# Three of five token blocks of the second expert turned by the DMA queue instead of the matrix engine

## The chip, the cores and the metric

The kernel runs on one core of one Trainium2 chip. Its time is device microseconds (us) of one execution. Before the change three runs gave 709.59, 711.19 and 712.39 us; the median is 711.19 us. One more execution was profiled, and all durations below are from it.

The engines are named as in the profile: PE is the matrix engine, PEld its weight loads, DVE the vector engine, ACT the scalar engine, POOL GpSimd, SP the engine that issues most DMAs. A `q` behind a name (SPq) is the engine's instruction queue, where DMAs are issued.

## The reference

The first half is attention over 8 batches, 8 heads, 576 positions and 64 values a head: a softmax over positions averaged by four, repeated four times, plus a softmax over the neighbours with |i - j| < 4. The sum, 4608 tokens of 512 values, is `x` of the second half, a mixture of eight experts with room for 576 tokens each:

```python
logits = x @ w_gate
order = np.argsort(-flat)                    # best pair of token and expert first
for idx in order:
    tok, e = (int(idx) // E, int(idx) % E)
    if assigned[tok] >= 0 or counts[e] >= cap:
        continue
    assigned[tok] = e
    counts[e] += 1
for e in range(E):
    mask = assigned == e
    h = np.maximum(x[mask] @ w1[e], 0.0)     # 576 x 512 by 512 x 1024
    out[mask] = h @ w2[e]                    # 576 x 1024 by 1024 x 512
```

## The kernel before

**Stages.** Attention writes `x` to DRAM (`x_dram`) and the logits to SBUF. Then a routing phase finds which expert fills up first and the numbers of its 576 tokens; each later phase finds the next expert and runs beside the previous expert's matmuls. Experts run one after another. "The second expert" below is the one with `i == 1` in the loop of `moe_attention`; its tokens and weights are fetched and prepared while the first expert's last matmuls run.

**One expert.** `weights` loads 4 MB on SP's queue; `split` makes of each piece two fp16 parts, `wh` (ACT, L1200) and the remainder `wl` (DVE, L1202, two instructions of 512 columns a piece). `gather` fetches the tokens' rows in five blocks (four of 128 rows and one of 64) into `xg` by indirect DMA from POOL (L1217). A block must be turned, so that the 512 values lie on the partitions, and split into a high and a remainder part, giving `xt`. There are two ways. `piece` turns a block on PE, four 128x128 fp32 transposes (L1234) into PSUM, and then ACT writes the high part (L1238) and DVE the remainder (L1239). `piece_dma` splits first, ACT (L1245) and DVE (L1246) into `xs`, and then SP issues one DMA that turns both parts (L1248). Experts one and two use `piece`, the others `piece_dma`.

**The two layers.** In `mlp` the first layer goes over eight slices `f` of 128 hidden columns. Each has two sums in PSUM tile `pH`, over tokens 0 to 255 (12 matmuls of 256 columns, L1279) and over tokens 256 to 575 (12 matmuls of 320 columns). The 12 are four slices of the depth by three products: high by high, high weight by remainder of x, remainder of the weight by high x. The list `seq` takes the three products in turn for each slice of depth. The list `late`, used by the first expert for `f < 2`, takes the four high products first, then the four with the weight's remainder, then the four with x's remainder; there the sums over 256 tokens of `f` 0 and 1 come before both sums over 320. The results go to `ht`, high part by ACT (L1303), remainder by DVE (L1306). The second layer goes over the five blocks `c` (L1320) into `pX`, ACT scales into `y` (L1327), for block 4 DVE adds its second half (L1329), POOL scatters the rows (L1330).

**What sets the order.** Each engine takes its instructions in program order, and a scheduler places them by priority and by the hints in the code. `in2` says behind which block of the previous expert's second layer the next expert's blocks are prepared: for the first expert the table `GET0` says blocks 0 and 1 behind block 3, blocks 2 to 4 behind block 4. The routing phase's own matmuls on PE (L871 counts against thresholds `level` or `cmp`, L889 and L917 broadcasts) stand between the layers' matmuls; each L871 waits for a compare on DVE (L822, which makes `cmp`), and the next L889 waits for three `less` and one `flag` on DVE (L881, L884). `val` and `ol` (L905, L1051) close the first count and start the second.

Of the kernel before, what the change touches and what calls it, by code (L numbers as in the profile page):

```python
# [734 lines left out]
W1S, W2S, XM = 64.0, 64.0, 8.0  # L735
# [413 lines left out]
class Experts:  # L1149
# [58 lines left out]
    def gather(self, idx, first, second=False):  # L1208
# [15 lines left out]
        def piece(c):  # L1224
# [12 lines left out]
            with self.tc.high_priority():  # L1237
                nc.scalar.activation(hi, p[:, :, :n], AF.Copy, scale=XM)  # L1238
                self.lows.append(nc.vector.scalar_tensor_tensor(lo, p[:, :, :n], XM, hi, op0=OP.mult, op1=OP.subtract))  # L1239

        def piece_dma(c):
            s0, n = SL[c]
            xs = self.wk.tile([128, 2, HD], F16, name="xs", bufs=XSB)
            with self.tc.high_priority():
                nc.scalar.activation(xs[:n, 0], xgs[c][:n], AF.Copy, scale=XM)  # L1245
            getattr(nc, LOE).scalar_tensor_tensor(xs[:n, 1], xgs[c][:n], XM, xs[:n, 0], op0=OP.mult, op1=OP.subtract)  # L1246
            with self.tc.high_priority():
                self.sent = nc.sync.dma_start_transpose(xt[:, :, :, s0:s0 + n].rearrange("p a d s -> p (a d) s"),  # L1248
                                            xs[:n].rearrange("p a d -> p (a d)"))

        return xt, piece if first or second else piece_dma

# [8 lines left out]

    def mlp(self, w, xt, idx, in1, in2, first=False):
        nc = self.nc
# [12 lines left out]
        def product(f, p, s):  # L1276
            s0, s1 = CUT[s]
            for j, (d, a, b) in enumerate(late if first and f < 2 else seq):
                mm = nc.tensor.matmul(p[:, s, :s1 - s0], w[d][a][:, 128 * f:128 * f + 128], xt[:, b, d, s0:s1],  # L1279
                                      start=j == 0, stop=j == len(seq) - 1)  # L1280
                self.products.append(mm)
                mark(mm, (s1 - s0) / 2400)
            return mm

        ph = {}
        for f in range(8):
            for z in (0, 1) if first and f == 0 else () if first and f == 1 else (f,):
                ph[z] = self.ps.tile([128, 2, 512], F32, name="pH", bufs=2)
# [53 lines left out]
GET = {0: (0, 1), 1: (2, 3), 2: (4,)}  # L1342
GET0 = {3: (0, 1), 4: (2, 3, 4)}
BEHIND = ((1, 6), (2, 2))
# [10 lines left out]
def moe_attention(tc, q, k, v, wg, w1, w2, cst, out):  # L1355
    nc = tc.nc
    with ExitStack() as top:
# [13 lines left out]
        with ExitStack() as ctx:  # L1371
# [21 lines left out]
            for i in range(E):  # L1393
# [29 lines left out]

                ex.mlp(w, xt, idx, in1, in2, i == 0)
                if i == 0:
# [66 lines left out]
```

## Time and profile before

| | us |
|---|---|
| median of three runs | 711.19 |
| the profiled execution | 709.79 |
| its span, first to last instruction | 708.1 |
| PE busy in the span | 649.8 (92%) |
| DVE busy | 533.6 (75%) |
| ACT busy | 337.7 (48%) |

The profiled execution took 1.69 us more than its span and lies 1.40 us under the median. By stage, PE is busy 222.42 of the first 250 us (attention), 14.13 of the next 30 (first routing phase, clock granted 0.61 of full speed on average), 65.47 of 280 to 347 (first expert), 55.68 of 347 to 405 (second expert) and 292.12 of 405 to 698 (the other six). Busy means that at least one instruction of the engine is under way; matmuls overlap, so the distance between two starts tells more than a duration. In the rows below the number in brackets is the idle time of the engine before an instruction, and what released it. A granted clock of 1.00 is 2.4 GHz, 0.50 is 1.2 GHz.

### The profile page before, as it was taken

Reading aid. Unit: us, or ns where it says so; the run is one execution under the profiler, and the core shown is the slowest. Engines: PE = TensorE matmul, PEld = TensorE weight load, DVE = VectorE, ACT = ScalarE, POOL = GpSimd, SP = SyncE. Lnnn points to the kernel's source line nnn. Section 1 sums busy time; section 2 is a strip of 40 time slices with the busy share of each in tenths; the row PEclk is TensorE's granted clock in tenths of the full one; section 3 lists DMA queues with packets and bytes.
Section 4 is the critical chain, followed back from the end, with each engine's and each line's share of the span. In section 5 each row is a group of like instructions: output and inputs, shape, how many; then the busy total and the mean of one; then the engine's idle time right before and its main releaser. Section 6 shows DMA issues by size and latency. Waiting matters only on the chain.

```text
span 708.1 us, 21934 instructions
## 1 busy us (share of the span) xinstructions
PE 649.8 (92%) x8938; PEld 451.0 (64%) x8938; DVE 533.6 (75%) x1562; ACT 337.7 (48%) x650; POOL 232.7 (33%) x303
## 2 busy tenths in 40 slices
PE   6888999889999845999999999999999999999994
PEld 4667878778787733774574575575674674755741
DVE  5798889987989977887889697797797876634500
ACT  4567778787785521532532443443444424424410
POOL 4865374644737420402402303204104106202011
PEclk9899999999999975999999999999999999999997
DMA  9967859777785632605507617638348269814001
GB/s 263 245 157 218 227 159 245 205 205 202 197 238 160 192 117 89 218 1 181 192 1 283 157 43 269 129 116 229 95 183 204 55 233 198 313 35 100 1 31 38
DMA packets 132157, 113.73 MB, mean 161 GB/s; under 512 B 81240, under 2 KB 109912, under 8 KB 132056
## 3 DMA queue, kind: packets, MB, share of 16 engines
q1 hardware_dynamic: 124760, 90.76, 45.0%
q0 software_dynamic: 6432, 20.98, 9.5%
q8 instruction: 71, 1.16, 0.7%
q10 hardware_dynamic: 864, 0.58, 0.3%
q14 instruction: 30, 0.25, 0.1%
HBM read 85.74 MB, written 19.46 MB: 149 GB/s over the span
## 4 chain that ended last, share of the span: by engine, by line
PE 45%; DVE 22%; issue 17%; ACT 5%; DMA 5%; POOL 4%; SPq 1%; ACTq 0%; POOLq 0%; DVEq 0%
PE pH L1279 13%; PE pX L1320 11%; PE g L574 3%; PE pR L871 2%; DVE wl L1202 2%; PE g L327 2%; POOL out_dram L1330 2%; DVE x L453 2%; PE g L552 2%; PE g L592 2%; PE s L532 1%; DVE qt L311 1%; POOL xg L1217 1%; PE g L407 1%; PE pH L1186 1%
## 5 line engine op out<-in xcount | busy, mean ns | idle before, releaser
L1279 PE MATMUL pH<-xt,wh 128*128 128x256 f16 (+1 forms) x1024 | 191.3, 286 | 1.2 <-ACT xt L1238 0.5
L1320 PE MATMUL pX<-wh,ht 128*128 128x512 f16 (+1 forms) x640 | 178.0, 379 | 0.0
L1279 PE MATMUL pH<-xt,wl 128*128 128x320 f16 (+1 forms) x512 | 144.6, 286 | 0.0
L1320 PEld LDWEIGHTS <-ht 128*128 128x128 f16 (+1 forms) x960 | 82.6, 100 | 93.9 <-issue 3.8
L1320 PE MATMUL pX<-wl,ht 128*128 128x512 f16 (+1 forms) x320 | 117.6, 379 | 0.0
L1279 PEld LDWEIGHTS <-wh 128*128 128x128 f16 x1024 | 97.5, 98 | 30.2 <-issue 5.7
L1330 POOL DMA_INDIRECT out_dram<-y,idx x40 | 43.0, 1074 | 177.8 <-ACT y L1327 153.5
L1303 ACT ACTIVATE ht<-pH 128x512 f16<-128x512 f32 (+1 forms) x128 | 45.5, 407 | 112.5 <-PE pH L1279 112.5
L1202 DVE SCALAR_TENSOR_TENSOR wl<-nat,wh 128x512 f16<-128x512 f32 x128 | 83.5, 687 | 14.9 <-ACT wh L1200 8.3
L1327 ACT ACTIVATE y<-pX 128x512 f32<-128x512 f32 (+1 forms) x40 | 23.8, 594 | 103.4 <-PE pX L1320 54.3
L1306 DVE SCALAR_TENSOR_TENSOR ht<-pH,ht 128x512 f16<-128x512 f32 (+1 forms) x128 | 52.3, 450 | 24.4 <-ACT ht L1303 23.9
L1200 ACT ACTIVATE wh<-nat 128x1024 f16<-128x1024 f32 x64 | 67.3, 1053 | 4.1 <-DMA nat<-in_moe_w_dram 4.1
L1217 POOL DMA_INDIRECT xg<-x_dram,idx x40 | 42.5, 1062 | 61.9 <-DVE used L1100 33.4
L1279 PEld LDWEIGHTS <-wl 128*128 128x128 f16 x512 | 49.9, 98 | 12.7 <-issue 0.8
L563 ACT COPY pt<-g 64x512 f32<-64x512 f32 x72 | 41.8, 581 | 28.8 <-PE g L552 27.8
L574 PE MATMUL g<-vw,pt 128*64 128x65 f32 x1152 | 45.5, 229 | 5.6 <-issue 2.7
L574 PEld LDWEIGHTS g<-vw,pt 128*64 128x64 f32 x1152 | 39.6, 142 | 12.7 <-issue 6.6
L327 PE MATMUL g<-ident,nat 128*128 128x128 f32 x256 | 40.4, 283 | 3.9 <-DMA nat<-in_q_dram 3.3
L313 ACT COPY kt<-g 64x512 f32<-64x512 f32 (+1 forms) x60 | 38.3, 639 | 6.2 <-PE g L327 5.2
L1246 DVE SCALAR_TENSOR_TENSOR xs<-xg,xs 128x512 f16<-128x512 f32 (+1 forms) x30 | 20.3, 688 | 26.8 <-ACT xs L1245 15.7
L1019 POOL MEMSET f<- 128x1 bf16 x8 | 0.8, 106 | 116.3 <-DVE sumf L925 44.2
L300 POOL TENSOR_TENSOR gtmp<-kt 128x576 f32<-128x576 f32 x14 | 16.1, 1147 | 61.4 <-ACT kt L313 43.6
(221 smaller groups left out, 1153.0 us busy)
## 6 DMA issues: line engine op xcount, KB each, us to landing
nat<-in_moe_w_dram SPq DMA_DIRECT2D x28, 1024.0 KB
vw<-in_v_dram SPq DMA_DIRECT2D x136, 78.0 KB
x_dram<-x SPq DMA_DIRECT2D x36, 256.0 KB
nat<-in_q_dram SPq DMA_DIRECT2D x32, 256.0 KB
nat<-in_k_dram SPq DMA_DIRECT2D x32, 256.0 KB
nat<-in_v_dram SPq DMA_DIRECT2D x28, 256.0 KB
up<-up_dram SPq DMA_DIRECT2D x9, 256.0 KB
nat<-in_moe_w_dram SPq DMA_DIRECT2D x4, 512.0 KB
```

The costliest lines, as they stand in the source:

```text
L313: self.nc.scalar.copy(out, in_)
L327: nc.tensor.transpose(p[:, a, :, fp], src[:, 4 * hh + 2 * a + s, 2 * fp:2 * fp + 2].rearrange("p f d -> p (f d)"), self.ident)
L563: self.nc.scalar.copy(out, in_)
L574: nc.tensor.matmul(o[64 * i:64 * i + 64, 65 * h:65 * h + 65], pt[:, 2 * (h % 2) + i, 2 * g + h // 2].rearrange("p b q -> p (b q)"), self.v ...
L1200: nc.scalar.activation(hi, r, AF.Copy, scale=sc)
L1202: nc.vector.scalar_tensor_tensor(lo[:, a:a + LOP], r[:, a:a + LOP], sc, hi[:, a:a + LOP], op0=OP.mult, op1=OP.subtract)
L1217: self.fetched = nc.gpsimd.indirect_dma_start(out=xg[:n], out_offset=None, in_=self.x, in_offset=bass.IndirectOffsetOnAxis(ap=idx[:n, c:c ...
L1279: mm = nc.tensor.matmul(p[:, s, :s1 - s0], w[d][a][:, 128 * f:128 * f + 128], xt[:, b, d, s0:s1], start=j == 0, stop=j == len(seq) - 1)
L1303: last = nc.scalar.activation(hi, q, AF.Relu)
L1306: low = nc.vector.scalar_tensor_tensor(lo, q, 0.0, hi, op0=OP.max, op1=OP.subtract)
L1320: mm = nc.tensor.matmul(p[o:o + m], ht[:, f, h0:h0 + m], w[4 + f // 2][b][:, 512 * (f % 2):512 * (f % 2) + 512], start=j < parts, stop=j > ...
L1330: i = nc.gpsimd.indirect_dma_start(out=self.out, in_=y[:n], in_offset=None, out_offset=bass.IndirectOffsetOnAxis(ap=idx[:n, c:c + 1], axis=0))
```

## The change

Blocks 2, 3 and 4 of the second expert are prepared by `piece_dma`; blocks 0 and 1 stay with `piece`. All five are now asked for behind block 3 of the first expert's second layer (`GET0`). A hint keeps ACT's part of `piece_dma` behind the high part of block 1. And the second expert too uses the order `late` for `f < 2`, with both sums over 256 tokens ahead of both sums over 320. Behind the edits every line number of the changed kernel is larger: L1279 is L1284 there, L1246 is L1249, L1248 is L1251, L1306 is L1311, L1329 is L1334.

```diff
-                nc.scalar.activation(hi, p[:, :, :n], AF.Copy, scale=XM)
+                self.high = nc.scalar.activation(hi, p[:, :, :n], AF.Copy, scale=XM)
...
         def piece_dma(c):
...
-                nc.scalar.activation(xs[:n, 0], xgs[c][:n], AF.Copy, scale=XM)
+                half = nc.scalar.activation(xs[:n, 0], xgs[c][:n], AF.Copy, scale=XM)
+            if second:
+                self.tc.add_manual_dep(half.ins, self.high.ins.name, mybir.DependencyInfo(
+                    mybir.DependencyClass.NoSync, mybir.DependencyReason.DATA), reason="behind")
...
-        return xt, piece if first or second else piece_dma
+        if first:
+            return xt, piece
+        return xt, (lambda c: (piece_dma if c in SENT2 else piece)(c)) if second else piece_dma
...
-    def mlp(self, w, xt, idx, in1, in2, first=False):
+    def mlp(self, w, xt, idx, in1, in2, first=False, two=False):
...
-            for j, (d, a, b) in enumerate(late if first and f < 2 else seq):
+            for j, (d, a, b) in enumerate(late if two and f < 2 else seq):
...
-            for z in (0, 1) if first and f == 0 else () if first and f == 1 else (f,):
+            for z in (0, 1) if two and f == 0 else () if two and f == 1 else (f,):
...
-GET0 = {3: (0, 1), 4: (2, 3, 4)}
+GET0 = {3: (0, 1, 2, 3, 4)}
+SENT2 = (2, 3, 4)
...
-                ex.mlp(w, xt, idx, in1, in2, i == 0)
+                ex.mlp(w, xt, idx, in1, in2, i == 0, i < 2)
```

On PE, where the second expert's first layer begins, the kernel before has this; `wh_6902` to `wh_7014` are the four depth slices of its weights, `level_82` the thresholds of the routing phase that runs beside it.

```order
L1234 MATMUL pH<-ident,xg 128x128 x4
L1234 MATMUL pX<-ident,xg 128x64 x4
L871 LDWEIGHTS level_82
...
L1279 MATMUL pH<-xt,wl_6969 128x256
L1234 MATMUL pH<-ident,xg 128x128 x4
L1279 LDWEIGHTS wh_7014
...
L889 MATMUL pR<-flag_5872,one 128x8
...
L1279 MATMUL pH<-xt,wl_7015 128x256
L1279 LDWEIGHTS wh_6902
L1279 MATMUL pH<-xt,wh_6902 128x320
```

Blocks 2 and 4 are turned ahead of the first layer, block 3 inside the first sum, and the sum over 320 tokens follows after 12 matmuls of 256 columns. In the changed kernel the same engine has, from the end of the first layer's 24th matmul of 256 columns:

```order
L1284 MATMUL pH<-xt,wh_7026 128x256
L871 LDWEIGHTS cmp_7116
L871 MATMUL pR<-oh,cmp_7116 128x32
...
L889 LDWEIGHTS one
L889 MATMUL pR<-flag_5874,one 128x8
L1284 LDWEIGHTS wh_6902
L1284 MATMUL pH<-xt,wh_6902 128x320
```

The three turns are gone, the 18 matmuls on `level_82` have moved up behind the turn of block 1, and nine L871 and one L889 of the next routing step stand together between the last 256-column and the first 320-column matmul. Before, these nine stood behind 12 matmuls of 256 columns and 7 of 320, and the L889 another 3 and 5 later. From the nine L871 on `cmp_7217` on (the second compare after `ol`) the routing's matmuls stand behind the same numbers of layer matmuls in both kernels.

On DVE the stretch from the remainder of block 1 on is, as a difference:

```order
 L1239 SCALAR_TENSOR_TENSOR xt<-pH,xt 128x4x128
-L1329 SCALAR_TENSOR_TENSOR y<-pX,y 64x512
...
 L881 TENSOR_TENSOR less<-cap,pR 64x8
+L1249 SCALAR_TENSOR_TENSOR xs<-xg,xs 128x512
 L884 TENSOR_TENSOR flag_5872<-pR,less 64x8
...
+L1249 SCALAR_TENSOR_TENSOR xs<-xg,xs 128x512
+L1334 SCALAR_TENSOR_TENSOR y<-pX,y 64x512
 L894 TENSOR_REDUCE nj<-pR 128x1
...
+L1249 SCALAR_TENSOR_TENSOR xs<-xg,xs 64x512
```

The remainders of blocks 2, 3 and 4 now stand among the routing step's small operations, the 64-row block behind the addition for `y`, and all of them ahead of the threshold and the compare that make `cmp_7116`. On SP the three turning DMAs stand behind the second expert's four weight loads and ahead of the third expert's.

## Rows read from the trace of the kernel before

**Rows 1.** Timeline of PE: start, us, engine, line, operation, [idle before <-releaser].
```profile
343.44 0.66 PE L1234 MATMUL pH<-ident,xg 128*128 128x128 f32 x4
...
345.66 0.66 PE L1234 MATMUL pH<-ident,xg 128*128 128x128 f32 x4
...
346.63 0.62 PE L871 MATMUL pR<-oh,level 128*128 128x16 bf16 x18
347.10 0.38 PE L1279 MATMUL pH<-xt,wh 128*128 128x256 f16 x2
...
348.08 0.60 PE L1234 MATMUL pH<-ident,xg 128*128 128x128 f32 x4
...
349.36 0.30 PE L1279 MATMUL pH<-xt,wh 128*128 128x320 f16 x1 [0.33 <-ACT xt L1238]
350.09 0.30 PE L1279 MATMUL pH<-xt,wh 128*128 128x320 f16 x1 [0.43 <-DVE xt L1239]
...
350.90 0.38 PE L871 MATMUL pR<-oh,cmp 128*128 128x32 bf16 x9
...
352.13 0.17 PE L889 MATMUL pR<-flag,one 128*128 128x8 bf16 x1
...
359.29 0.60 PE L871 MATMUL pR<-ol,level 128*128 128x16 bf16 x18 [0.19 <-DVE ol L1051]
```

**Rows 2.** Timeline of DVE, same stretch.
```profile
344.85 0.68 DVE L1239 SCALAR_TENSOR_TENSOR xt<-pH,xt 128x512 f16<-128x512 f32 x1
...
350.05 0.75 DVE L822 TENSOR_TENSOR cmp<-xh,thr 128x1152 bf16<-128x1152 int16 x1
351.32 0.16 DVE L881 TENSOR_TENSOR less<-cap,pR 32x8 f32<-32x8 f32 x1 [0.51 <-PE pR L871]
...
351.90 0.15 DVE L884 TENSOR_TENSOR flag<-pR,less 32x8 bf16<-32x8 f32 x1
...
358.94 0.30 DVE L1051 TENSOR_TENSOR ol<-oh,e 128x288 bf16<-128x288 bf16 x1
```

**Rows 3.** Timeline of ACT, same stretch.
```profile
345.81 0.59 ACT L1327 ACTIVATE y<-pX 64x512 f32<-64x512 f32 x1 [1.08 <-PE pX L1320]
...
352.01 0.71 ACT L1303 ACTIVATE ht<-pH 128x512 f16<-128x512 f32 x2 [2.69 <-PE pH L1279]
```

**Rows 4.** Instructions that write tiles xs and xt by the DMA way: ns min/median/max.
```profile
L1245 ACT ACTIVATE xs<-xg x30: 612/629/631, 388.1 to 643.2; 128x512 f16<-128x512 f32 x24, 64x512 f16<-64x512 f32 x6
L1246 DVE SCALAR_TENSOR_TENSOR xs<-xg,xs x30: 683/688/693, 388.7 to 643.8; 128x512 f16<-128x512 f32 x24, 64x512 f16<-64x512 f32 x6
L1248 SPq DMA_TRANSPOSE xt<-xs x30: 1222/1293/2304, 389.5 to 644.6; - x30
```

**Rows 5.** Timeline of SP: the last 64-row turn, issued alone.
```profile
644.56 1.22 SPq L1248 DMA_TRANSPOSE xt<-xs  x1
```

**Rows 6.** Last busy quarter microsecond of its transfer: busy by engine, clock, DMA share, GB/s.
```profile
646.50:646.75 0.25, 0.25 (x3) 0.10 (x1) 0.00 (x0) 0.00 (x0) 0.00 (x0) 1.00 0.64 93
```

**Rows 7.** Half microseconds at a gather's end, same columns.
```profile
387.50:388.00 0.50, 0.50 (x4) 0.22 (x3) 0.41 (x4) 0.00 (x0) 0.33 (x1) 1.00 0.03 8
```

**Rows 8.** Timeline of ACT: waits for a gather and for a turning DMA.
```profile
388.06 0.63 ACT L1245 ACTIVATE xs<-xg 128x512 f16<-128x512 f32 x1 [4.97 <-DMA xg<-x_dram,idx]
...
446.10 0.63 ACT L1245 ACTIVATE xs<-xg 64x512 f16<-64x512 f32 x1 [0.80 <-DMA xt<-xs]
```

**Rows 9.** Timeline of SP: the five turns of the fourth expert.
```profile
439.70 9.25 SPq L1248 DMA_TRANSPOSE xt<-xs  x5
```

**Rows 10.** Timeline of PE: one long wait in the attention stage.
```profile
67.92 0.66 PE L552 MATMUL g<-ident,sw 128*128 128x128 f32 x4 [1.68 <-ACT sw L544]
```

**Rows 11.** Half microseconds behind it, and a microsecond with PE idle elsewhere, columns of Rows 6.
```profile
69.00:69.50 0.50, 0.50 (x38) 0.42 (x26) 0.48 (x2) 0.47 (x2) 0.50 (x1) 0.50 1.06 365
...
72.00:72.50 0.50, 0.50 (x14) 0.49 (x12) 0.43 (x3) 0.00 (x0) 0.50 (x1) 0.62 0.39 107
...
246.00:247.00 1.00, 0.00 (x1) 0.00 (x0) 1.00 (x1) 0.16 (x1) 0.93 (x1) 1.00 0.29 79
```

## The prediction

> **What bounds the kernel now.** I read the stages first (the table ahead), then PE's timeline where the second expert begins, then DVE's and ACT's beside it, then what the DMA way costs where other experts use it. PE is busy in 55.68 of the 58 us from 347 to 405, so what PE does or waits for there is time. PE turns block 1 from 343.44, blocks 2 and 4 from 345.66 to 346.63, does 18 routing matmuls until 347.10 and then starts the first layer; from 348.08 it turns block 3, and then it waits twice for that block, 0.33 us for ACT and 0.43 for DVE [rows 1]. These are the things that the change can take off PE. The next place where PE and DVE meet is the L871 on `ol` at 359.29, where PE had waited 0.19 us for DVE [rows 1]: DVE is as late as PE there. Whatever PE gains before has to pass that place too.
>
> **Part by part.**
>
> *Turns and stalls taken off PE.* Blocks 2 and 4 took 346.63 - 345.66 = 0.97 us, block 3 some 0.5 (a 128-row block, so a little over half of the 0.97), the two waits 0.76 [rows 1]. At most 0.97 + 0.5 + 0.76 = 2.2 us can be gained.
>
> *The start of the first layer.* From the turn of block 1 to the end of block 4 of the second layer PE took 345.66 - 343.44 = 2.22 us; the 18 L871 move in front of that end and keep their 347.10 - 346.63 = 0.47. The first layer so begins at 343.44 + 2.22 + 0.47 = 346.1, 1.0 earlier. Nine matmuls of 256 columns take 348.08 - 347.10 = 0.98, 0.109 each [rows 1], so the 24 that now come first take 2.6 and PE reaches the L871 on the first compare at 348.75.
>
> *The new wait for the compare.* DVE gets there by this chain: remainder of block 1 until 344.85 + 0.68 = 345.53 [rows 2]; `less`, 0.16; remainder of block 2, 0.69 [rows 4], until 346.35; `flag`, 0.15; block 3 until 347.05. Then the addition for `y` stands in front: ACT's `y` was at 345.81 and comes 0.47 later, until 346.87 [rows 3], so no wait, and it ends at 347.7; `nj`, block 4 until 348.35, the threshold, the compare from 348.5 for 0.75 [rows 2]. The L871 starts 0.10 after the compare's end as before (350.05 + 0.75 against 350.90), at 349.35. PE waits 348.75 to 349.35, 0.6 us. ACT hides its three L1245 of 0.63 [rows 4] in idle time; if it were late, each microsecond would be paid in this chain. The L889 behind it follows the nine L871 at 352.13 - 350.90 = 1.23 us, the time that DVE needs for three `less` and the `flag` (351.32 to 352.05) [rows 1, 2]. Before, matmuls of the layer stood between the two; now only the L871 themselves do, some 0.4. That is another 0.8 us of waiting. PE is free for the 320-column matmuls at 349.35 + 1.23 = 350.6.
>
> *The new wait for the three DMAs.* The trace has none of them beside so little traffic, so I bound it. SP can issue block 2 at 346.45, and one issue takes 1.29 [rows 4], so block 4, ready on DVE at 348.35, is issued at 349.0. The lone 64-row turn was issued at 644.56 and its last busy quarter ended at 646.75, 2.2 us later, beside a scatter as here [rows 5, 6]. The last bytes move by 349.0 + 2.2 = 351.2. A waiting engine hears of it later: a gather had stopped moving at about 387.5, and ACT started on it at 388.06, 0.56 later [rows 7, 8]. From below the wait is nothing (landed by 350.6, for which the bytes would have to move in 1.6 us); from above it is the fourth expert's case, where block 0, first issued at 439.70, let ACT go only at 446.10, 6.4 us later, between gathers and scatters [rows 8, 9]. Here the gathers are done when the turns start. I take the lone one, with half of the gather's lag: 351.5, a wait of 0.9 us.
> The Trainium skill, "DMA: Bandwidth & Descriptors", section "Anatomy of one DMA — SWDGE (gpsimd) path", says that a DMA's semaphore moves only once its last byte is confirmed at the target, and puts most of a fixed cost of about 2.0 us there. By an estimate from that page the 320-column matmuls would start up to 1.5 us after my 351.5; the 0.56 of the gather speaks for a smaller lag, and no run here shows the turn's own.
>
> *From there to `ol`, on PE.* Before, PE needed from the L889 at 352.13 to 359.10 (359.29 less the wait) 6.97 us, for 28 matmuls of 256 and 24 of 320 columns by the order of before. Now 19 and 36 are left, 1536 columns more, 6 x 0.109 = 0.65 us. PE is at the place at 351.5 + 6.97 + 0.65 = 359.1, as before.
>
> *From there to `ol`, on DVE.* The first slice's 12 matmuls of 320 columns take 12 x 0.136 (0.109 x 320 / 256) and 0.23 for nine L871 among them, so ACT's first eviction starts 2.05 after 351.5, at 353.55. Before, it went from that eviction at 352.01 to `ol` at 358.94, 6.93 us [rows 2, 3]; a compare (0.75) and four small operations (0.7) of that now stand ahead of the eviction, so 5.5 are left. `ol` starts at 359.05, and the L871 0.35 later, at 359.4, 0.1 later than before. PE waits 0.3 for it.
>
> *Behind it* the routing's matmuls come back to the same places of the order, so I let the shift stand: PE is busy 292.12 of the last 293 us, and a shift goes to the end whole. Three more PSUM reads fall away on DVE and three L1246 come; that is inside the chains above.
>
> *The sum.* 1.0 gained by the earlier start and 0.76 by the old waits, and 0.5 by block 3; paid again with 0.6 and 0.8 for the compare and the flag, 0.9 for the DMAs and 0.3 at `ol`, less the 0.2 that PE waited there: about +0.1 us on the profiled execution's 709.79, 709.9. The median of the runs lies 1.4 higher, so 711.3 there.
>
> **The rivals.**
>
> *The DMAs land in time* (at 350.6 or before). For it: a lone 64-row turn needed only 2.2 us. Against it: three issues of 1.29 stand one behind another. DVE's chain to `ol` then starts 0.9 earlier and the end is at 710.4. If moreover DVE had the compare before PE came, all 2.2 us would be gained: 709.0.
>
> *The clock falls.* From 348.75 to 351.5 PE only does nine small L871 and one L889. In the attention stage PE waited 1.68 us before 67.92 [rows 10], and the clock was at its lower level (0.50, 1.2 GHz) from 69.0 until within 72.0 to 72.5 [rows 11], although PE was busy all that time. A whole microsecond of idle at 246 left it at 1.00 [rows 11]. The stretch here is longer than the first with some work in it. About 3.2 us at half the rate cost 1.6 us of PE's work; 0.3 of it hides in the wait for `ol`, and the second slice's eviction comes late for DVE. The end is at 711.3 + 1.3 = 712.6.
> The Trainium skill, "TensorE: Matmul & The Clock Gate", section "What's actually happening", says that the gate runs free of the kernel, so that where a fall comes differs from run to run; by that the same stretch can cost 1.3 us in one run and nothing in the next, and no row here shows one place in two runs.
>
> *The DMAs land as late as in the fourth expert.* The place is the wait of the first 320-column matmul on block 4. With 6.4 us from issue the data come at 349.0 + 6.4 = 355.4, 3.9 later than I take, and all of it goes to the end: 715.2, with the clock's fall 716.5. It decides (0.5% of the time, 3.6 us) from a landing at about 355. Against it: in the fourth expert four more blocks, gathers and scatters moved in those microseconds.
>
> **How the numbers follow.** The forecast, no change to within 0.7 us, has 0.5; the clock's fall 0.25; DMAs in time 0.17; DMAs as late as in the fourth expert 0.08. A median of three runs that spread from 709.59 to 712.39 adds about 1 us either way. The range goes from 709.1 (all of the gain) to 713.8 (the clock's fall and the spread). A measurement of this kernel can tell about 0.5%, 3.6 us, from no change. Faster by more would need 707.6, which is under every gain that I can find: 0.03. Slower by more, 714.8, is the last rival: 0.08. The rest, 0.89, is the same.
>
> **What would show it.** In the profile after, the first 256-column matmul stands 1 us earlier against the turn of block 1; PE shows waits before the nine L871 (about 0.6, by DVE's `cmp`), before the L889 (0.8, by `flag`) and before the first 320-column matmul (0.9, by the DMA); the L871 on `ol` comes at about 359.4, PE waiting for DVE; the granted clock stays at 1.00 around 352 to 356. I am wrong if the 320-column matmuls start at once behind the L889, if the L871 on `ol` moves by more than 0.7 us, or if the shift there isn't the shift at the end.

## The result and the profile after

The changed kernel takes 720.0 us in the median of four runs (717.5 to 722.6) against 711.8 of the kernel before beside it: ratio 1.0145, 95% interval 1.0099 to 1.0191. I had forecast 711.3, no change, with a range from 709.1 to 713.8. One traced execution below, of late_gather, took 1053 us at a granted clock of 0.556, so its trace is left out. The profiled execution took 722.63 us, its span 721.0, 12.9 more than the 708.1 of before. I take "T0", the turn of the second expert's block 0 on PE (341.33 before, 343.74 after), as zero: ahead of it both kernels do the same work in the same order, so the 2.4 us until there are scatter between executions. The other 10.5 lie in two places, 2.8 between T0 and the L871 on `ol` and 8.0 in the third expert; the rest gives 0.4 back.

*The second expert.* PE's timeline after (start, us, engine, line, operation, [idle before <-releaser]), to be held beside [rows 1]:

```profile
343.74 0.66 PE L1234 MATMUL pH<-ident,xg 128*128 128x128 f32 x4
346.13 0.66 PE L1234 MATMUL pH<-ident,xg 128*128 128x128 f32 x4 [0.32 <-DVE xt L1239]
346.62 0.60 PE L871 MATMUL pR<-oh,level 128*128 128x16 bf16 x18
...
352.31 0.39 PE L871 MATMUL pR<-oh,cmp 128*128 128x32 bf16 x9 [0.71 <-DVE cmp L822]
...
353.54 0.17 PE L889 MATMUL pR<-flag,one 128*128 128x8 bf16 x1 [0.83 <-DVE flag L884]
...
355.60 1.25 PE L1284 MATMUL pH<-xt,wh 128*128 128x320 f16 x4 [1.90 <-DMA xt<-xs]
...
364.53 0.60 PE L871 MATMUL pR<-ol,level 128*128 128x16 bf16 x18 [0.17 <-DVE ol L1051]
```

The waits for `cmp` and `flag` are as forecast (0.6 and 0.8), the one for the DMAs (the turns) is 1.90 instead of 0.9. From the turn of block 1 to the L871 on `ol` it takes 18.40 us, before 15.85 [rows 1]: 2.55 more. SP's timeline has the three turns in one row, and the windows (busy time of PE, PEld, DVE, ACT and POOL, each with its number of instructions in brackets, then granted clock, DMA share, GB/s) show when their bytes move, and the clock:

```profile
349.13 4.12 SPq L1251 DMA_TRANSPOSE xt<-xs  x3
```
```profile
350.00:350.50 0.50, 0.50 (x7) 0.44 (x6) 0.50 (x1) 0.00 (x0) 0.00 (x0) 1.00 0.05 9
350.50:351.00 0.50, 0.50 (x7) 0.45 (x5) 0.47 (x3) 0.00 (x0) 0.15 (x1) 1.00 1.08 206
352.00:354.00 2.00, 0.56 (x10) 0.32 (x10) 1.12 (x7) 0.00 (x0) 0.14 (x1) 1.00 1.03 182
354.00:355.00 1.00, 0.00 (x0) 0.00 (x0) 0.92 (x3) 0.00 (x0) 0.00 (x0) 0.92 0.76 130
355.00:355.50 0.50, 0.00 (x0) 0.00 (x0) 0.00 (x0) 0.00 (x0) 0.00 (x0) 0.50 0.02 3
355.50:358.00 2.50, 2.40 (x10) 1.37 (x11) 0.00 (x0) 0.00 (x0) 0.00 (x0) 0.50 0.00 0
358.00:359.00 1.00, 1.00 (x16) 0.81 (x15) 0.48 (x3) 0.14 (x1) 0.00 (x0) 0.87 0.00 0
```

The first bytes move 1.4 us after the first issue, the last ones until about 355, and PE goes on 0.6 later. While PE stood still, the granted clock fell from 1.00 to 0.50 (1.2 GHz).

*The third expert.* Nothing was edited there, and I had let the shift stand. PE, after:

```profile
390.71 0.62 PE L871 MATMUL pR<-oh,level 128*128 128x16 bf16 x18 [0.50 <-DVE oh L993]
...
409.08 0.17 PE L889 MATMUL pR<-flag,one 128*128 128x8 bf16 x1 [6.44 <-DVE flag L884]
...
417.99 0.61 PE L871 MATMUL pR<-ol,level 128*128 128x16 bf16 x18
```

and before:

```profile
385.38 0.61 PE L871 MATMUL pR<-oh,level 128*128 128x16 bf16 x18 [0.51 <-DVE oh L993]
...
404.62 0.54 PE L871 MATMUL pR<-ol,level 128*128 128x16 bf16 x15
```

That is 27.28 us against 19.24, 8.04 more. Most of it is the wait of 6.44 us for `flag`. Behind it the clock had fallen here too:

```profile
409.00:412.50 3.50, 3.42 (x10) 1.07 (x11) 2.38 (x7) 0.28 (x2) 0.00 (x0) 0.50 0.48 116
```

Half a clock for some 3.5 us costs about 1.7 us by estimate, which accounts for the rest. Why PE waits for `flag` is seen on DVE: the last block's split (L1249, 64 rows) stands ahead of it,

```profile
408.15 0.69 DVE L1249 SCALAR_TENSOR_TENSOR xs<-xg,xs 64x512 f16<-64x512 f32 x1 [1.48 <-ACT xs L1245]
408.87 0.15 DVE L884 TENSOR_TENSOR flag<-pR,less 32x8 bf16<-32x8 f32 x1
```

and that split waits for ACT, and ACT for the last gather, whose data came 11.4 us after its issue at 396.06 (for the 1.90 and 4.40 us before that the profile names no releaser):

```profile
398.16 0.63 ACT L1245 ACTIVATE xs<-xg 128x512 f16<-128x512 f32 x1 [1.90 <-issue]
404.14 0.63 ACT L1245 ACTIVATE xs<-xg 128x512 f16<-128x512 f32 x1 [4.40 <-issue]
407.49 0.63 ACT L1245 ACTIVATE xs<-xg 64x512 f16<-64x512 f32 x1 [2.24 <-DMA xg<-x_dram,idx]
```

The DMA queues (packets, MB, share of 16 engines) in the four microseconds from 398.7, after:

```profile
DMA packets 729, 0.35 MB, mean 87 GB/s; under 512 B 687, under 2 KB 687, under 8 KB 728
...
q1 hardware_dynamic: 678, 0.17, 87.1%
q0 software_dynamic: 50, 0.17, 55.7%
```

and at the same distance from the first L871, from 393.4, before:

```profile
DMA packets 3004, 1.01 MB, mean 251 GB/s; under 512 B 2936, under 2 KB 2936, under 8 KB 3004
...
q1 hardware_dynamic: 2904, 0.73, 99.1%
q0 software_dynamic: 100, 0.28, 17.7%
```

The packets take up more of the engines' time than before (143% against 117%; the shares are sums over packets and can pass 100%) and move a third of the bytes: on average a packet takes 1.43 x 16 x 4 / 729 = 0.125 us instead of 0.025. Turns (q1: 0.082 instead of 0.022 us) and gathers and scatters (q0: 0.71 instead of 0.11) are held up together. It isn't that each packet is slower, though. In the traces' packet records the median of the turns' 256-byte packets is 0.018 us in both windows, that of the 4 KB packets of q0 0.186 us after and 0.159 before; but after, 19 packets took over 1 us, the longest 2.96, and make up nearly half of the time (42 of 92.5 us), and before none took over 0.33. This is called the stall below. Behind the third expert nothing is lost: from its L871 on `ol` to the end it is 303.0 us, before 303.5.

### The profile page after: what moved, and what is told of

Read it like the earlier page. It is cut to its first block, busy times and chain, and to the rows that moved or that the text cites. A ratio compares the mean times of both kernels' runs of the same rounds, so it can differ in the third digit from the quotient of the medians.

```text
span 721.0 us, 21917 instructions
## 1 busy us (share of the span) xinstructions
PE 652.7 (91%) x8926; PEld 452.1 (63%) x8926; DVE 533.0 (74%) x1562; ACT 337.7 (47%) x650; POOL 232.8 (32%) x303
## 4 chain that ended last, share of the span: by engine, by line
PE 45%; issue 18%; DVE 17%; ACT 8%; DMA 6%; POOL 4%; SPq 1%; ACTq 0%; POOLq 0%; DVEq 0%
PE pX L1325 13%; PE pH L1284 12%; PE g L574 3%; PE g L327 2%; POOL xg L1217 2%; PE pR L871 2%; DVE wl L1202 2%; PE g L552 2%; POOL out_dram L1335 2%; DMA xg<-x_dram,idx 2%; PE s L532 2%; ACT kt L313 1%; PE g L592 1%; ACT qt L313 1%; ACT pt L563 1%
## 5 line engine op out<-in xcount | busy, mean ns | idle before, releaser
L1284 PE MATMUL pH<-xt,wh 128*128 128x256 f16 (+1 forms) x1024 | 190.6, 286 | 2.3 <-DMA xt<-xs 1.9
L1284 PE MATMUL pH<-xt,wl 128*128 128x320 f16 (+1 forms) x512 | 143.3, 287 | 0.0
L1284 PEld LDWEIGHTS <-wh 128*128 128x128 f16 x1024 | 97.6, 98 | 32.9 <-issue 5.2
L1311 DVE SCALAR_TENSOR_TENSOR ht<-pH,ht 128x512 f16<-128x512 f32 (+1 forms) x128 | 52.3, 449 | 26.6 <-ACT ht L1308 26.2
L1200 ACT ACTIVATE wh<-nat 128x1024 f16<-128x1024 f32 x64 | 67.3, 1053 | 4.3 <-DMA nat<-in_moe_w_dram 4.2
L1284 PEld LDWEIGHTS <-wl 128*128 128x128 f16 x512 | 50.0, 98 | 12.3
L1249 DVE SCALAR_TENSOR_TENSOR xs<-xg,xs 128x512 f16<-128x512 f32 (+1 forms) x33 | 22.3, 687 | 34.8 <-ACT xs L1245 34.6
```

The lines of the kernel that those rows point to most:

```text
L1200: nc.scalar.activation(hi, r, AF.Copy, scale=sc)
L1311: low = nc.vector.scalar_tensor_tensor(lo, q, 0.0, hi, op0=OP.max, op1=OP.subtract)
```

## The experiments

All times in this table come from traces: from T0 to the L871 on `ol`; the third expert, from its first L871 on `oh` to that on `ol`; PE's wait for `flag` in it; the time from issue to landing of its last gather; and from T0 to the span's end, which leaves out the scatter ahead of T0. Ratios are those of whole runs to runs of before, with their interval.

```
               T0-ol  third  flag   landing  T0-end  ratio
before         17.96  19.24  -      <4.2     366.8
after          20.79  27.28  6.44   11.4     377.3   1.0145 [1.0099, 1.0191]
after_again    21.03  26.30  4.72   9.6      376.5   1.0104 [1.0039, 1.0169]
after_p3       20.90  23.90  3.23   8.1      374.7
hold_turns     20.79  20.75  -      4.0      370.8   1.0065 [1.0036, 1.0094]
hold_c1        21.74  20.75  1.70   6.5      372.6   1.0084 [1.0055, 1.0113]
getx3          20.98  19.47  -      7.7      370.4   1.0081 [1.0044, 1.0118]
getx3_p2       20.94  23.41  2.42   9.0      374.5
one_block_get  20.18  25.04  4.36   9.3      375.1   1.0117 [1.0072, 1.0162]
one_block      *      20.36  0.56   4.6      369.3   1.0022 [0.9986, 1.0057]
fill15         19.47  24.08  3.41   7.1      372.7   1.0114 [1.0068, 1.0161]
fill           *      21.21  -      5.4      368.2   1.0013 [0.9982, 1.0044]
order_only     19.22  19.04  -      <4.6     367.4   1.0060 [1.0030, 1.0090]
order_p2       20.83  19.93  0.89   4.7      369.9
late_only      *      20.30  0.73   5.4      366.5   0.9986 [0.9959, 1.0014]
late_gather2   17.97  18.95  -      3.8      365.9   1.0023 [0.9994, 1.0052]
later_gather   17.98  20.22  1.19   4.9      366.9
waste          19.36  20.07  1.04   5.3      368.5   1.0066 [1.0027, 1.0106]
waste_p2       21.46  18.88  -      4.1      369.4
```

(* there the L871 on `ol` has another place in PE's order. The ratio beside late_gather2 is that of the runs of late_gather, the same kernel. For before and order_only the trace gives no landing; their bound is the start of the split that needs the data. All columns but the ratio are of one execution each.)

**after_again, after_p3**, the changed kernel unedited. 

> The changed kernel once more, nothing edited. In its first trace the third expert, from its first L871 on oh to its L871 on ol, took 27.28 us against 19.24 before, and PE waited 6.44 us there for flag, because the last of five gathers landed 11.4 us after its issue. If that is a property of the order (its five turning DMAs always meet its gathers, or a later expert's turns are always slow behind the second expert's three), the stretch takes 25 to 28 us again and the time is 719 to 721. If it was one execution's chance, the stretch takes 19 to 21 us in this trace and this execution lies near 714. Either way the second expert's stretch, from the turn of block 1 to the L871 on ol, should take 18.4 us again (15.85 before), with PE waiting 1.9 us for the turning DMAs.

 

> The changed kernel, a third trace. In both traces so far the third expert's last gather landed late, with 4.7 and 6.4 us of PE's wait for flag, and the stretch took 27.3 and 26.3 us. If the stall belongs to this program's order and addresses, it is here again: 25 to 28 us. If it is drawn anew in each execution, as getx3 suggests (the same turns and gathers at the same times up to +5.8, no stall), 19 to 21 us are as likely.

 Measured: the stall is there each time, but its size is not fixed: the third expert takes 27.3, 26.3 and 23.9 us.

**hold_turns.** The third expert's turns wait for its last gather.

```diff
-XSB = 4
+XSB = 5
...
+            if hold:
+                self.tc.add_manual_dep(self.sent.ins, self.fetched.ins.name, ...Sync...)
...
-                    xt2, piece2 = ex.gather(idx2, False, i + 1 < ROWS)
+                    xt2, piece2 = ex.gather(idx2, False, i + 1 < ROWS, i == 1)
```

> The changed kernel, but the third expert's five turning DMAs are issued only when its last gather has landed, so that gathers and turns can no longer lie beside each other there (and xs has five buffers, so that the last block's split waits for no turn). Theory 1, the collision of gathers and turns: the gathers land within 4 us of their issue as before, PE's wait for flag falls from 6.44 to under 1 us, the third expert's stretch takes 19 to 21 us instead of 27.28, and the time is 712 to 715. Theory 2, that the second expert's three turns leave the queue in a state in which later turns crawl: the turns still take over 2 us each, the stretch stays above 24 us and the time at 718 or more.

 Measured: ACT has every block in time (beside the rows of after above),

```profile
395.25 0.63 ACT L1245 ACTIVATE xs<-xg 128x512 f16<-128x512 f32 x1 [0.88 <-ACT y L1335]
396.74 0.63 ACT L1245 ACTIVATE xs<-xg 128x512 f16<-128x512 f32 x1
398.29 0.63 ACT L1245 ACTIVATE xs<-xg 64x512 f16<-64x512 f32 x1 [0.43 <-ACT y L1335]
```

and the third expert takes 20.75 us. Without turns beside them the gathers don't stall (the last one lands in 4.0 us instead of 11.4), though the second expert's three turns are there: theory 1 holds in this, and theory 2, that later turns crawl by themselves, falls. The edit changes two things, the hold and the fifth buffer of `xs`; the fifth buffer was not run by itself. The 20.75 contain a new wait of 1.9 us for the late turns, and the runs take 715.7 in the median, a little over the 712 to 715 expected.

**hold_c1, getx3, one_block_get, fill15: what triggers it?** hold_c1 holds back the second turn alone, until the third gather has landed; getx3 moves the last block's split behind `flag`; one_block_get turns only block 3 of the second expert by DMA.

```diff
+            if hold and c == 1:
+                self.tc.add_manual_dep(self.sent.ins, fetched[2].ins.name, ...Sync...)
```
```diff
+GETX = {0: (0, 1), 1: (2, 3), 3: (4,)}
...
-                            for j in GET.get(c, ()) if i else ():
+                            for j in (GETX if i == 1 else GET).get(c, ()) if i else ():
```
```diff
-GET0 = {3: (0, 1, 2, 3, 4)}
-SENT2 = (2, 3, 4)
+GET0 = {3: (0, 1), 4: (2, 3, 4)}
+SENT2 = (3,)
```

> The changed kernel with one wait more: of the third expert's five turning DMAs only the second (block 1) waits until the third gather (block 2) has landed; every engine's order is that of the changed kernel. In the changed kernel this turn is issued at +5.82 us (counted from the expert's first L871 on oh), while GpSimd is still writing the last gather (+5.35 to +6.57); in the kernel before it comes at +6.13, after the last gather's issue (+5.16 to +6.07). Here it should come at about +7.2. If the collision hangs on this phase, the third expert's stretch takes 19 to 21 us (27.28 in the changed kernel), PE waits under 1 us for flag, and the time is 711 to 715. If any overlap of turns and gathers behind the second expert's three turns makes them crawl, holding one turn for 1.4 us changes little: 24 to 27 us, time 717 to 720.

 

> The changed kernel, but in the third expert the last block's split (ACT's and DVE's xs of 64 rows) stands two steps later, so that on DVE the flag that PE waits for no longer stands behind it. The collision itself stays. If PE's 6.44 us are due to DVE's order (flag behind a split whose gather is late), PE's wait for flag falls to about 2 us (the fourth block's split, ahead of flag still, ends at +14.8, against +18.2), and what is left comes back later as a wait for xt by the 320-column products: the stretch takes 22 to 25 us, the time is 714 to 718. If the late data bound PE anyway, the stretch stays at 26 to 28 us and the time at 719 to 721.

 

> getx3 once more (the last block's split two steps later). In its first trace the third expert took 19.5 us, though the second turn was issued at +5.77 as in the stalled traces. If moving the split removed the stall for good, the stretch takes 19 to 20 us again; if the stall is drawn anew in each execution, the fourth block's split may come at +12 or later here, and with flag behind it the stretch takes 22 us or more.

 

> The changed kernel with only block 3 of the second expert turned by DMA, and blocks 2 and 4 turned on PE behind the fourth block of the second layer, as before (in one_block they were turned one block earlier and PE waited 0.93 and 0.90 us for gathers, with the clock at 0.50 for 3 us behind it). Without these waits the stretch from the turn of block 0 to the third expert's first L871 should take 43 to 44.5 us (44.05 before, 45.95 in one_block), the third expert 19 to 20.5 us if the collision hangs on phase, and the time 709.5 to 711.5. If one turn in the second expert is enough to leave the queue in a slow state, the third expert takes over 22 us.

 Measured: the phase theory says that the stall hangs on when the second turn is issued against the last gather (times with a + count from the expert's first L871 on `oh`). hold_c1 came out as it said in the stretch, 20.75, but PE still waited 1.70 us for `flag` (expected: under 1) and the last gather took 6.5 us to land. In getx3's first trace the second turn went out at +5.77, as in the stalled traces, and the third expert took 19.47 us:

```profile
399.04 0.63 ACT L1245 ACTIVATE xs<-xg 128x512 f16<-128x512 f32 x1 [0.19 <-ACT wh L1200]
...
405.01 0.62 ACT L1245 ACTIVATE xs<-xg 64x512 f16<-64x512 f32 x1
```

The fourth block came in time (+8.1; after: +13.4). But the last gather landed 7.7 us after its issue, so the stall was there as well; the last split, now behind `flag`, held up nothing that PE waited for. In the second trace the fourth block came at +11.6 and `flag`, behind it, 2.42 us late; in after_again, with the fourth block at +11.9, `flag` came 4.72 late. So the two traces show what the order on DVE costs, and don't speak against the phase theory. fill15 (below) does: it stalled, with a landing of 7.1 us, with the second turn at +7.67, behind the last gather's issue. So the issue of that turn is not the trigger. one_block_get (landing 9.3 us, all four runs at 719.4 to 720.6) shows that one turn in the second expert is enough; my expectation of a time like before's was wrong by 8 us.

**late_gather, late_gather2, later_gather**: before, with one or two memsets on GpSimd ahead of the third expert's last gather. 

> The kernel before, nothing of the change in it, but a memset of 128x640 on GpSimd (about 0.6 us by the 0.95 of one of 128x1024) between the third expert's fourth and fifth gather; every other engine's order is that of before. The last gather is so issued at about +5.8 instead of +5.16, and the second turn at +6.13 falls into its issue. If the stall of the third expert is a collision that hangs on this phase, it appears here too, without any turn in the second expert: the stretch takes 23 to 28 us instead of 19.24, PE waits several us for flag, and the time is 715 to 720. If the second expert's turns are needed for it, or the exact phase doesn't matter, the stretch takes 19 to 20.5 us and the time is that of before.

 

> late_gather once more, for a profile at the usual clock (its times, 712.3 against 710.8, already speak against a stall of 8 us). In the runs so far the third expert stalled where its second turn was issued at +5.7 to +5.8 us, 0.5 to 0.9 us before the end of the last gather's issue, and not where it came at +6.1 or later, after that end. Here the last gather's issue should lie at about +5.8 to +6.7 and the turn at +6.1. If the stall hangs on the turn falling into that issue, the stretch must take over 23 us in this trace as well; if it hangs on the turn's time against the gathers before, it takes 19 to 20.5 us.

 

> The kernel before with two memsets of 128x640 on GpSimd between the third expert's fourth and fifth gather, so that the last gather's issue begins at about +6.4, after the second turn's (+6.1) has begun. If two turns ahead of the last gather are what makes both crawl, the stretch takes over 23 us; if not, 20 to 21.5 us (the last gather simply comes 1.2 us later).

 Measured: no stall. In late_gather2 the second turn shifted too (+7.18), so the case wasn't made; in later_gather it went out at +6.69, inside the last gather's issue (+6.54 to +7.45), and the third expert took 20.22. That the turn falls into this issue is thus not enough for a stall either, at least without turns in the second expert.

**waste, waste_p2**: before, with three turns more on SP's queue that nobody reads.

```diff
+                    t = nc.sync.dma_start_transpose(waste[:, :, 64 * j:min(64 * j + 64, 160)], w[0][0][:64 if j < 2 else 32])
...
```

> The kernel before and nothing of the change, but three turning DMAs more on SP's queue in the second expert (64, 64 and 32 rows of weights, 40% of the bytes of the changed kernel's three, into a tile that nobody reads), issued where the first layer begins, about where the changed kernel issues its own; every engine's order is else that of before. If turns in the second expert are by themselves what lets the third expert's gathers stall 20 us later, its stretch takes 22 us or more here (19.24 before; 23.9 to 27.3 in the changed kernel) and the time is 714 to 720. If it needs more than that (the later arrival of PE and of the routing, the order on DVE), the stretch takes 19 to 20.5 us and the time is that of before.

 

> The same kernel, a second trace, since the stall differs from one execution to the next: 22 us or more again for the third expert if the second expert's turns alone make it, 19 to 20.5 us if not.

 Measured: the turns went out earlier than meant, at 332.30, in the first expert, so the case wasn't made. Two of the second expert's weight loads, behind them on SP's queue, went out at 336.51 only (before: all four from 326.33 on), and the second expert's last gather came late:

```profile
332.30 3.95 SPq L1295 DMA_TRANSPOSE waste<-wh  x3
```
```profile
347.41 0.43 PE L1234 MATMUL pX<-ident,xg 64*128 64x64 f32 x4 [1.36 <-DMA xg<-x_dram,idx]
```

In waste_p2 that wait is 1.96 us. The third expert did not stall. Turns earlier on the queue are thus not sufficient, at least at this distance and with 40% of the bytes. The ratio of 1.0066 (4.7 us) is more than these two traces account for: +1.7 and +2.6 us from T0 to the end, with +1.4 and +3.5 of it up to the L871 on `ol`; that stays open.

**order_only, order_p2, late_only, one_block: the rest of the change without the turns.** order_only has `SENT2 = ()`; one_block `SENT2 = (3,)`, both with the changed GET0 (so one_block keeps one turn); late_only is before with `i < 2` for the order of the sums, and nothing else.

```diff
-                ex.mlp(w, xt, idx, in1, in2, i == 0)
+                ex.mlp(w, xt, idx, in1, in2, i == 0, i < 2)
```

> The changed kernel with all five blocks of the second expert turned on PE; the order of the products in its first two sums stays as changed. If the three turning DMAs of the second expert cost what the traces show (1.9 us of PE's wait there, the fall of the clock behind it, and by either theory the third expert's 8 us), the second expert's stretch takes 15 to 16 us, the third expert's 19 to 20 us, and the time is 710.5 to 712.5, as before. If the order of products has a part in it (PE's two waits for cmp and flag, 0.71 and 0.83, and the clock), the second expert's stretch stays at 17 us or more and the time above 713.

 

> order_only once more (no turning DMA in the second expert). If turns in the second expert are needed for the stall, the third expert takes 19 to 20 us again; if the stall is drawn anew in each execution for any order, it may take 23 us or more here.

 

> The changed kernel with only block 3 of the second expert turned by DMA; blocks 2 and 4 are turned on PE as before. One turn alone is issued some 1.3 us earlier than the last of three and should have landed before the 320-column matmuls need it: the second expert's stretch takes 15 to 16 us. For the third expert, theory 1 (collision by phase) expects 19 to 21 us, since the phase is nearly that of before, and a time of 710 to 712.5; theory 2 (turns leave the queue in a slow state) expects some of the loss, 21 us or more, and 713 to 720.

 

> The kernel before with one part of the change alone: the second expert's first two sums run in the new order (256 tokens of both first, the products with the remainders last); all its blocks are turned on PE where they were turned before. From the turn of block 0 to the third expert's first L871 on oh it took 44.05 us before and 46.97 in the changed kernel. If the order by itself is harmless (my prediction put its two waits for cmp and flag at 1.4 us against 1.26 of old waits and room), the stretch takes 43.5 to 44.5 us, the third expert 19 to 20.5, and the time is that of before. If the order has a price, it shows as waits for cmp or flag before the first layer's 320-column matmuls and the stretch takes 45 us or more.

 Measured: the new order of the sums alone costs nothing (366.5 from T0 to the end, ratio 0.9986, interval 0.9959 to 1.0014); in none of these four does the third expert stall. In order_only and one_block the blocks behind block 0 are turned too early for their gathers. order_p2:

```profile
346.49 0.66 PE L1234 MATMUL pH<-ident,xg 128*128 128x128 f32 x4 [1.08 <-DMA xg<-x_dram,idx]
347.88 0.43 PE L1234 MATMUL pX<-ident,xg 64*128 64x64 f32 x4 [0.73 <-ACT xt L1238]
```
```profile
350.00:353.00 3.00, 3.00 (x14) 1.38 (x14) 1.45 (x3) 1.20 (x2) 0.00 (x0) 0.52 0.00 0
```

There the clock falls to 0.52 behind the two waits, in order_only's first trace, with waits of 0.96 and 0.78, it stays at 1.00; from T0 to the L871 on `ol` that makes 1.6 us between two executions of one kernel (19.22 and 20.83). It may be part of why order_only's runs are 0.6% slow where I expected none; the rest of that is open, since the two traces lie only 0.6 and 3.1 us above before from T0 to the end.

**fill, fill15: PE's waits in the second expert.** Matmuls into a half sum that is overwritten later fill them; the output is the same.

```diff
+            if two and not first and f == 0:
+                for j in range(FILL):
+                    mm = nc.tensor.matmul(p[:, 1, :256], w[0][0][:, :128], xt[:, 0, 0, :256], start=True, stop=True)
+                    self.products.append(mm)
```

> The changed kernel with 30 matmuls of 256 columns more in the second expert (0.109 us each, into a half of the sum that is overwritten later; they change no result): 6 ahead of the L871 on cmp, 9 ahead of the L889 on flag, 15 ahead of the first 320-column products, to fill PE's three waits of 0.7, 0.8 and 1.9 us. If the fall of the clock to 0.50 behind these waits costs the second expert about 1.0 us, the clock stays at 1.00 here, and from the turn of block 0 to the L871 on ol it takes 19.6 to 20 us instead of 20.8 to 21.0. If the clock falls all the same or the fillers cost as much as they save, it takes 20.6 us or more. The third expert's stall is not touched by it (26 to 28 us, or less if its phase moves).

 

> fill with 15 of its 30 additional matmuls: 6 ahead of the L871 on cmp and 9 ahead of the L889 on flag, none ahead of the first 320-column products. So PE's waits for cmp and flag are filled, the wait for the turning DMAs, about 1.9 us, is left. If that wait alone brings the clock down, it is at 0.50 for some 2 us behind it, as in the changed kernel, and from the turn of block 0 to the L871 on ol it takes 20.5 to 21 us (20.8 to 21.0 in the changed kernel). If the two waits ahead of it are needed for the fall, the clock stays at 1.00 and it takes 19.7 to 20.1 us.

 Measured, fill15:

```profile
354.21 1.14 PE L1298 MATMUL pH<-xt,wh 128*128 128x256 f16 x9
355.20 0.17 PE L889 MATMUL pR<-flag,one 128*128 128x8 bf16 x1
357.33 0.72 PE L1284 MATMUL pH<-xt,wh 128*128 128x320 f16 x4 [1.96 <-DMA xt<-xs]
```
```profile
353.50:355.50 2.00, 1.73 (x23) 1.18 (x20) 1.13 (x6) 0.00 (x0) 0.31 (x1) 1.00 0.98 186
355.50:357.50 2.00, 0.17 (x2) 0.14 (x3) 1.08 (x4) 0.00 (x0) 0.00 (x0) 1.00 0.48 75
357.50:360.50 3.00, 3.00 (x32) 2.24 (x31) 1.00 (x5) 1.10 (x3) 0.00 (x0) 1.00 0.00 0
```

Behind the DMA wait of 1.96 alone the clock stays at 1.00 in this trace; it fell in all seven traces in which the two others stand ahead of it unfilled (in one_block_get behind two, of 0.82 and 1.25). But it does not follow that the two are needed. In waste_p2 PE waits once, just as long, and the clock falls behind it:

```profile
345.34 0.43 PE L1234 MATMUL pX<-ident,xg 64*128 64x64 f32 x4 [1.96 <-DMA xg<-x_dram,idx]
```
```profile
346.00:349.00 3.00, 3.00 (x27) 2.44 (x24) 0.75 (x3) 0.20 (x1) 0.00 (x0) 0.50 0.22 61
```

From T0 to the L871 on `ol` fill15 takes 19.47, 1.4 less than the changed kernel's 20.9 (mean of three): that is the fall's price there. It can be more: in hold_c1 the clock was low for about 6.8 us instead of 3.4, and the same stretch took 21.74. In fill the three waits are gone (PE is busy in 8.76 of the 9 us from 347 to 356, at 1.00), the third expert takes 21.21 (its gathers start at other times there), and from T0 to the end it is 1.4 us more than before, although 30 x 0.109 = 3.3 us of it are matmuls for nothing. By this estimate, from one trace of each, the change takes some 1.9 us (3.3 - 1.4) off PE, and puts waiting in their place.

## Why the prediction was wrong

*Right:* the first layer starts 2.66 us behind the turn of block 1 (348.79), as worked out; the waits for `cmp` and `flag` (0.71 and 0.83 for 0.6 and 0.8); the gain of at most 2.2 on PE (1.9 by the estimate from fill). Of the signs that I had named for being wrong, two came: the L871 on `ol` moved by 2.55 us, and the shift there isn't the shift at the end.

*The new wait for the three DMAs* was mis-sized, 0.9 for 1.90. I took the landing 2.5 us behind the last issue, from a lone 64-row turn. The last issue came at 351.99, PE went on at 355.60: 3.6. One 128-row turn alone, in one_block_get, needs 3.25 from issue to PE:

```profile
351.68 1.38 SPq L1251 DMA_TRANSPOSE xt<-xs  x1
```
```profile
354.93 0.44 PE L1284 MATMUL pH<-xt,wh 128*128 128x320 f16 x2 [1.25 <-DMA xt<-xs]
```

Its bytes move from about 353.0 to 354.3 (1.3 us ahead, 1.3 of transfer, 0.6 behind). In the changed kernel three turns move without a gap from 350.5 to 355, so the last one also waits for the bytes of those ahead: the term that I left out. The rule that I had cited from the Trainium skill ("DMA: Bandwidth & Descriptors", section "Anatomy of one DMA — SWDGE (gpsimd) path") puts most of a fixed 2.0 us behind the last byte. It is written for DMAs that GpSimd issues; for these turns, which SP issues, the rows show 0.6 there and more of the rest ahead of the first byte.

*The clock falls* was a rival with 0.25. It did fall, each time; its price, 1.4 by fill15, is what I had put (1.3 to the end). I gave it too little: I had PE nearly idle from 348.75 to 351.5, 2.75 us, and with the longer wait for the turns it was 4.0 us, from 351.6 to 355.6. The Trainium skill ("TensorE: Matmul & The Clock Gate", section "What's actually happening") has the gate run free of the kernel. order_only and order_p2 agree with that, one place falling in one execution and not in the next, and so do single waits of 1.96 us in fill15 and waste_p2, but at the three waits it did not vary.

*"Behind it the routing's matmuls come back to the same places of the order, so I let the shift stand"* is the step that failed, by 8.04 us of the 10.5. The order on PE came back as I said, but the shift did not stand: in the third expert PE waits 6.44 us for `flag`, behind a gather that the turns beside it hold up for 11.4 us. In the kernel before the third expert's turns ran beside its gathers at 251 GB/s, and I did not ask whether that would last. The rival with DMAs "as late as in the fourth expert" spoke of such traffic, gave it 0.08 and placed it in the second expert, where the gathers are done. The sum lacked no more than 2.4 us in the second expert: 1.0 for the turns, 1.4 for the clock.

*What stays open.* Shown: the gathers and turns of the third expert hold each other up (with the turns held back in hold_turns the last gather lands in 4.0 us, in the changed kernel in 8.1 to 11.4); the size differs between executions of one kernel (third expert 23.9 to 27.3; 19.5 and 23.4); and PE pays for it through a split that stands ahead of `flag` on DVE. All seven traces of after, one_block_get, getx3 and fill15 have a landing of 7.1 us or more; all eight without turns in the second expert one of 5.4 or less; one_block and fill, with turns there but gathers that start at other times, 4.6 and 5.4; hold_c1, with one turn held, lies between with 6.5 (the gaps are narrow, and each trace is one execution). Not shown: by what the second expert's turns bring this about. The time of the second turn, the last gather's issue and earlier turns on the queue were each tried, and none alone does it. Nor does it lie in the buffers alone: `xs` has four that are used in turn, so each turn in the second expert shifts which of them the third expert's blocks get, but one_block shifts them as one_block_get does and fill as fill15 does. No version that beats the kernel before came out of this; late_only is even with it.

## What to carry to other kernels

Moving work from an engine to a DMA queue isn't done where the data land: look at the next place where that queue and another one serve the same engine, and ask what has kept them from holding each other up so far. Count a chain of DMAs by issue, transfers in a row and lag, not by the last one alone; and price a stretch of waits in a row as one, with the clock's fall: it came behind three waits in seven traces of seven, behind a single one of 1.96 us in one of two. A wait for a gather ahead of a small flag on an in-order engine turns a late transfer into an idle TensorE: hold the turns until the gathers have landed (27.3 to 20.8 us here), or put the split behind the flag (19.5 and 23.4).

## What the runs showed of the hardware that I had not expected

Turning DMAs and indirect gathers at once can slow each other to 87 GB/s at full engine share, with a gather landing 11.4 us after its issue; without turns beside it (hold_turns) the last one, issued at 394.22, landed in 4.0. The typical packet is no slower for that; a few are held for 1 to 3 us. In 17 traces (all but the two of waste) T0 comes at 340.3 to 349.0 us, though the kernels have the same order of work ahead of it: whole runs of one kernel scatter by more than the effects in question, and a fixed instruction as zero was needed to see them.
